# Order of the first loads and first token passes in a SwiGLU feed-forward kernel

## The chip, the core and the metric

The kernel runs on one core of one Trainium2 chip. The core has a matrix engine (TensorE; PE in the profile, with PEld for its weight loads), a vector engine (DVE), a scalar engine (ScalarE, ACT), GpSimd (POOL) and a sync engine (SyncE, SP), each with its own instruction queue. Engines wait for each other by semaphores. SyncE and ScalarE both start DMA transfers here; an issue occupies the queue of the engine that makes it, and the transfer's landing is told by a semaphore of its own. The metric is the device time of one execution in microseconds (us), the median of several.

## The reference

With x of 2048 tokens by D = 512, weights w_gate and w_up of 512 by F = 1376, and w_down of 1376 by 512, all bf16:

```
def reference(x, w_gate, w_up, w_down):
    g = _silu(x @ w_gate)
    u = x @ w_up
    return (g * u) @ w_down
```

## The kernel before

Tokens are worked on in four chunks of 512, F in ten tiles of 128 and a remainder of 96. For each chunk and F tile TensorE makes two groups: G, the tile's columns of w_gate times the tokens, and U, the same of w_up. A group is four accumulating matmuls (D is cut into four parts of 128, index `dk`) into one of eight PSUM banks, used in rotation. ScalarE takes the SiLU of G into a buffer; VectorE multiplies this by U into `hT_sb`, the input of the second product, which follows when all chunks are done. The remainder of F has groups X and Y of its own, and the second product the functions `strips` and what follows it. Neither is touched here.

The weights arrive in slabs of F tiles: (0), (1), (2, 3), (4, 5, 6), (7 to 10). `load_gate` and `load_up` load a slab of w_gate or w_up; in the text wg2 is the gate slab that begins with tile 2, wu2 the up slab. Tokens 0 to 255 are loaded as rows (`load_xn`, two tiles of 128 tokens), transposed by TensorE (`transposes`) and copied from PSUM to `xT_sb` by VectorE and ScalarE in turn, four copies each. All other tokens come by transposing DMAs (`load_x`): x0b brings tokens 256 to 383, x0c 384 to 511, x1 to x3 the other chunks.

SyncE issues nearly all loads, in the written order of `loads_on_sync` (L123): xn0, wu0, wg1, wu1, wg2, wu2, x0b, x0c, wg4, wu4, wg7, wu7, then the rest. ScalarE issues wg0 and xn1 in `loads_on_scalar` (L119), loads its table, and then runs `act_ops` in order (L278); the first four of these are its copies of token tiles 0 and 1, two of each.

TensorE's order is written out by hand, and so is each wait: `gu_needs` (L329) waits for the loads that a pass needs, `gu_step` (L339) issues one matmul over tokens n0 to n1 and, for tokens 0 to 255, waits for the copies. The first eight groups (G0, U0, G1, U1, G2, U2, G3, U3, in the text by kind and F tile; `first` in the code) are cut by tokens, since the tokens of chunk 0 do not come at once:

- warm-up matmuls, transposes of token tile 0, G0 on tokens 0 to 127, transposes of tile 1, U0 on 0 to 127, then G0 and U0 on 128 to 255 (L371 to L378);
- G1, U1, G2, G3, U2, U3 on tokens 0 to 255 (L379);
- G0, U0 on 256 to 383, then on 384 to 511 (L381);
- the other six on 256 to 511 (L384).

From group 8 (G4) on every matmul spans 512 tokens. A G or U group is handed to its reader when its last matmul is done.

Of the kernel before, what the change touches and what calls it, by code (L numbers as in the profile page):

```python
# [14 lines left out]
def bass_standalone__swiglu_ffn__prompt_kernel(nc, x, w_gate, w_up, w_down, out):  # L15
# [3 lines left out]
    KD = D // P  # L19
# [3 lines left out]
    SC = 512  # L23
# [5 lines left out]
    HT = SC // 2  # L29
# [21 lines left out]
    with ExitStack() as es:  # L51
# [32 lines left out]
        def load_sem(name):  # L84
            loads[name] = sem(f"s_{name}")
            return loads[name]
# [6 lines left out]
        def load_x(eng, name, t0, t1):  # L93
            eng.dma_start_transpose(
                xT_sb[:, :, t0:t1], xf[t0:t1, :]
            ).then_inc(load_sem(name), 16)

        def load_w(eng, name, src, base, f0, f1):
            eng.dma_start(
                w_sb[:, :, base + f0:base + f1],  # L100
                src[:, f0:f1].rearrange("(k p) f -> p k f", p=P),
            ).then_inc(load_sem(name), 16)

        slabs = [(0, 1), (1, 2), (2, 4), (4, 7), (7, NFT)]
        slab_of = {ft: a for a, b in slabs for ft in range(a, b)}

        def load_gate(eng, a, b):
            load_w(eng, f"wg{a}", w_gate, 0, a * P, min(b * P, F))

        def load_up(eng, a, b):  # L110
            load_w(eng, f"wu{a}", w_up, UPH, a * P, min(b * P, F - 32))

        def load_xn(eng, i):
            eng.dma_start(xn_sb[:, i, :], xf[i * P:(i + 1) * P, :]).then_inc(load_sem(f"xn{i}"), 16)
# [4 lines left out]
        def loads_on_scalar(act):  # L119
            load_gate(act, *slabs[0])  # L120
            load_xn(act, 1)

        def loads_on_sync(sp):  # L123
            load_xn(sp, 0)
            load_up(sp, *slabs[0])
            for a, b in slabs[1:3]:
                load_gate(sp, a, b)
                load_up(sp, a, b)
            load_x(sp, "x0b", HT, HT + P)
            load_x(sp, "x0c", HT + P, SC)  # L130
            for a, b in slabs[3:]:
                load_gate(sp, a, b)
                load_up(sp, a, b)
            load_w(sp, "wut", w_up, F - (F - 32), F - 32, F)
            for c in range(1, NSC):
                load_x(sp, f"x{c}", c * SC, (c + 1) * SC)
            sp.dma_start(
                wd_sb[:, 0:NFF, :], w_down[0:NFF * P, :].rearrange("(k p) d -> p k d", p=P)
            ).then_inc(load_sem("wd"), 16)
            load_sem("wdt")  # L140
            for y0 in (0, 64):
                sp.dma_start(wd_sb[y0:y0 + 64, T01, :], w_down[NFF * P:F - SR, :]).then_inc(loads["wdt"], 16)
            for x0 in range(0, P, SR):
                sp.dma_start(wd_sb[x0:x0 + SR, T2, :], w_down[F - SR:F, :]).then_inc(loads["wdt"], 16)
            sp.dma_start(wd_sb[0:F_LAST, TAIL, :], w_down[NFF * P:F, :]).then_inc(load_sem("wdl"), 16)
# [7 lines left out]
        def add_group(kind, **what):  # L153
            g = dict(kind=kind, at=len(groups), bank=banks[len(groups) % NB], readers=[], **what)
            groups.append(g)
            return g

        def add_op(eng, g, **what):
            n_read[eng] += 1
            op = dict(g=g, at=n_read[eng], **what)  # L160
            (act_ops if eng == "A" else dve_ops).append(op)
            g["readers"].append((eng, op["at"]))
            return op

        def tview(i, dk):
            return banks[KD * i + dk][:, 0:P // 2].bitcast(BF16)
# [47 lines left out]
        for i in range(NXN):  # L214
            for dk in range(KD):
                eng = "DA"[dk % 2]
                op = add_op(
                    eng, dict(readers=[]), kind="copy", ready=(s_X, KD * i + dk + 1),
                    out=xT_sb[:, dk, i * P:(i + 1) * P], src=tview(i, dk), stored=(None, 0),
                )  # L220
# [12 lines left out]
        for at, t in enumerate(tiles):  # L233
# [3 lines left out]
            for c0, c1 in parts:  # L237
                g = add_group("O", t=t, c0=c0, c1=c1)
                eng = "A" if at % 2 == 1 and c0 == 0 else "D"
                op = add_op(  # L240
                    eng, g, kind="copy", out=o_sb[ob][:, c0:c1], src=g["bank"][:, 0:c1 - c0],
                    stored=(s_out[ob], need),
                )
# [6 lines left out]
        def ready(op):  # L250
            return op["ready"] if "ready" in op else (s_P, op["g"]["at"] + 1)

        def store_tiles(eng, own):
            for o, t, c0, c1, ob, copied, n in stores:
                if o == own:
                    eng.wait_ge(s_A if copied == "A" else s_D, n)
                    eng.dma_start(out_rows(t)[:, c0:c1], o_sb[ob][:, c0:c1]).then_inc(s_out[ob], 16)

        def on_sync(sp):
            loads_on_sync(sp)  # L260
            store_tiles(sp, "S")
            for i in range(NOS):
                sp.wait_ge(s_out[i], 16 * n_store[i])
# [11 lines left out]
        def on_scalar(act):  # L275
            loads_on_scalar(act)
            act.activation(adummy[:, 0:4], zero_c, ACT.Silu)  # L277
            for op in act_ops:  # L278
                act.wait_ge(*ready(op))
                if op["kind"] == "silu":  # L280
                    if op["free"]:
                        act.wait_ge(s_D, op["free"])
                    fn = ACT.Silu
                else:
                    if op["stored"][1]:
                        act.wait_ge(*op["stored"])
                    fn = ACT.Copy
                act.activation(op["out"], op["src"], fn).then_inc(s_A, 1)  # L288
            store_tiles(act, "A")
# [13 lines left out]
        def on_tensor(pe):  # L303
# [25 lines left out]
            def gu_needs(g, n0, n1):  # L329
                c, ft = g["c"], g["ft"]  # L330
                if c > 0:
                    need(f"x{c}")
                if c == 0 and n1 > HT:
                    need("x0b")
                if c == 0 and n1 > HT + P:
                    need("x0c")
                need(("wg" if g["kind"] == "G" else "wu") + str(slab_of[ft]))

            def gu_step(g, dk, n0, n1):  # L339
                c = g["c"]  # L340
                col = (0 if g["kind"] == "G" else UPH) + g["ft"] * P
                if c == 0:
                    for i in range(n0 // P, min(n1 // P, NXN)):
                        after(*xt_ready[i, dk])
                ins = whole(g["bank"], dk, col, c, n0, n1)
                if n1 == SC and dk == KD - 1:
                    ins.then_inc(s_P, 1)

            def gu_matmuls(g, n0, n1):
                gu_needs(g, n0, n1)  # L350
                for dk in range(KD):
                    gu_step(g, dk, n0, n1)
# [17 lines left out]
            first = groups[0:NB]  # L370
# [5 lines left out]
            for dk in range(KD):  # L376
                for g in first[0:2]:
                    gu_step(g, dk, P, HT)  # L378
            for at in (2, 3, 4, 6, 5, 7):  # L379
                gu_matmuls(first[at], 0, HT)  # L380
            for n0, n1 in ((HT, HT + P), (HT + P, SC)):  # L381
                for g in first[0:2]:
                    gu_matmuls(g, n0, n1)
            for g in first[2:]:  # L384
                gu_matmuls(g, HT, SC)

            for g in groups[NB:NO]:
                free(g)
# [98 lines left out]
        on_sync(nc.sync)  # L487
        on_gpsimd(nc.gpsimd)
        on_scalar(nc.scalar)
        on_tensor(nc.tensor)  # L490
        on_vector(nc.vector)

# [27 lines left out]
```

## Time and profile before

| | |
|---|---|
| Median of 3 runs | 120.31 us (120.24 to 120.88) |
| The profiled execution | 119.89 us |
| Its span, first to last instruction | 118.6 us |
| TensorE busy | 115.9 us (98%), 1019 matmuls |
| VectorE busy | 38.0 us (32%) |
| ScalarE busy | 35.1 us (30%) |
| Granted TensorE clock | 1.0 of full |
| DMA moved | 8.83 MB |

The profile is of one execution. A line of a group gives the source line, the engine, the operation and what it writes and reads, then busy time and the idle time before it with what ended it. In the chain of work the path is followed back from the last instruction. In a timeline a row is a start, a duration and what ran, merged where the same instruction repeats; the idle time ahead of it stands in brackets. Matmuls are pipelined: one that follows another starts before the other ends, so that a busy share of 98% does not say that it works at its full rate, and the spacing of the starts says what a matmul costs. The time of a DMA issue (SPq, ACTq) is what it holds its queue, not how long the data take.

### The profile page before, as it was taken

To read this page: it belongs to the slowest core of one execution; us is meant where nothing else is said; L and a number is where in the kernel's file an instruction comes from. 1 tells how busy PE (TensorE), PEld (TensorE's weight loads), DVE (VectorE), ACT (ScalarE), POOL (GpSimd) and SP (SyncE) were. 2 spreads that over 40 slices of the span, in tenths; PEclk is the share of its full clock that TensorE was granted. 3 is DMA by queue.
4 is the path that set the end of the run, shared out by engine and by line. 5 is a ranking of instruction groups with operands and counts; after the bars stand their busy time and mean duration, and the time that the engine had idled before them with its cause. 6 is when DMAs were issued, how large, how long until landed. Compare 5 with 4: busy or idle time off the path is not lost.

```text
span 118.6 us, 2344 instructions
## 1 busy us (share of the span) xinstructions
PE 115.9 (98%) x1019; PEld 59.7 (50%) x1019; DVE 38.0 (32%) x60; ACT 35.1 (30%) x62; POOL 1.1 (1%) x7
## 2 busy tenths in 40 slices
PE   7999999999999999999999999999999999999993
PEld 2788444444444444444444444444444445885442
DVE  0206542444433444324444244360000044003321
ACT  3407334353244272343263432330000033003021
POOL 1000000000000000000000000010000000000000
PEclk9999999999999999999999999999999999999999
DMA  3999999991000000000000000000000017200612
GB/s 87 290 186 336 296 161 221 268 357 25 0 6 0 0 0 0 0 3 3 0 0 6 0 0 0 0 0 6 0 6 0 0 57 237 70 0 6 202 64 88
DMA packets 17642, 8.83 MB, mean 74 GB/s; under 512 B 10624, under 2 KB 17632, under 8 KB 17632
## 3 DMA queue, kind: packets, MB, share of 16 engines
q1 hardware_dynamic: 16816, 8.33, 27.3%
q10 hardware_dynamic: 816, 0.36, 1.1%
q8 instruction: 8, 0.13, 0.5%
q14 instruction: 2, 0.02, 0.0%
HBM read 4.75 MB, written 2.10 MB: 58 GB/s over the span
## 4 chain that ended last, share of the span: by engine, by line
PE 98%; DVE 0%; issue 0%
PE bank L324 62%; PE bank L442 25%; PE bank L481 7%; PE bank L356 2%; PE bank L404 2%; PE bank L365 1%; DVE o_sb L300 0%
## 5 line engine op out<-in xcount | busy, mean ns | idle before, releaser
L324 PE MATMUL bank<-xT_sb,w_sb 128*128 128x512 bf16 (+2 forms) x384 | 73.3, 352 | 0.1
L324 PEld LDWEIGHTS bank<-xT_sb,w_sb 128*128 128x128 bf16 x384 | 36.2, 98 | 36.8 <-DMA w_sb<-in_w_gate_dram 0.3
L296 DVE TENSOR_TENSOR hT_sb<-sg_sb,bank 128x512 bf16<-128x512 f32 x40 | 27.5, 688 | 40.2 <-PE bank L324 39.3
L288 ACT ACTIVATE sg_sb<-bank 128x512 f32<-128x512 f32 x40 | 23.9, 597 | 40.6 <-PE bank L324 40.5
L442 PE MATMUL bank<-wd_sb,hT_sb 32*128 32x512 bf16 x496 | 29.0, 374 | 0.0
L442 PEld LDWEIGHTS bank<-wd_sb,hT_sb 32*128 32x128 bf16 x496 | 15.2, 93 | 11.6 <-issue 0.4
L300 DVE CAST o_sb<-bank 128x512 bf16<-128x512 f32 (+1 forms) x10 | 5.7, 595 | 31.1 <-PE bank L442 25.9
L288 ACT ACTIVATE o_sb<-bank 128x512 bf16<-128x512 f32 (+1 forms) x8 | 4.3, 582 | 33.6 <-PE bank L442 27.9
L481 PE MATMUL bank<-wd_sb,hT_sb 128*128 128x512 bf16 (+2 forms) x56 | 8.1, 304 | 0.0
L481 PEld LDWEIGHTS bank<-wd_sb,hT_sb 128*128 128x128 bf16 x56 | 4.2, 98 | 4.2 <-issue 0.4
L442 PE MATMUL bank<-wd_sb,hy_sb 32*128 32x512 bf16 (+1 forms) x32 | 5.0, 371 | 0.0
L296 DVE TENSOR_TENSOR hx_sb<-sgx_sb,bank 32x512 bf16<-32x512 f32 x4 | 2.8, 692 | 3.5 <-ACT sgx_sb L288 3.5
L288 ACT ACTIVATE sgx_sb<-bank 32x512 f32<-32x512 f32 x4 | 2.4, 588 | 4.5 <-PE bank L324 4.5
L356 PE MATMUL bank<-const-bfloat16-1.0 128*128 128x512 bf16 (+1 forms) x9 | 2.8, 463 | 0.8 <-PEq L505 0.8
L442 PE MATMUL bank<-wd_sb,hx_sb 32*128 32x512 bf16 (+1 forms) x16 | 3.0, 371 | 0.0
L288 ACT ACTIVATE sgy_sb<-bank 64x512 f32<-64x512 f32 x4 | 2.4, 590 | 0.1
L356 PEld LDWEIGHTS bank<-const-bfloat16-1.0 128*128 128x128 bf16 x9 | 1.0, 128 | 2.2 <-issue 2.2
L300 DVE COPY xT_sb<-bank 128x128 bf16<-128x128 bf16 x4 | 0.8, 222 | 4.3 <-PE bank L365 4.3
L404 PE MATMUL bank<-xT_sb,w_sb 128*64 128x512 bf16 x16 | 1.9, 382 | 0.0
L442 PEld LDWEIGHTS bank<-wd_sb,hy_sb 32*128 32x128 bf16 x32 | 1.6, 93 | 0.6
L277 ACT ACT_TABLE_LOAD x1 | 1.3, 1283 | 1.9 <-issue 1.9
L404 PEld LDWEIGHTS bank<-xT_sb,w_sb 128*64 128x64 bf16 x16 | 0.8, 109 | 1.0 <-DVE hT_sb L296 0.4
(15 smaller groups left out, 6.6 us busy)
## 6 DMA issues: line engine op xcount, KB each, us to landing
out_dram<-o_sb SPq DMA_DIRECT2D x15, 128.0 KB, 1.8
wd_sb<-in_w_down_dram SPq DMA_DIRECT2D x1, 1280.0 KB, 7.3
w_sb<-in_w_gate_dram SPq DMA_DIRECT2D x1, 480.0 KB, 5.5
w_sb<-in_w_up_dram SPq DMA_DIRECT2D x1, 448.0 KB, 6.2
w_sb<-in_w_gate_dram SPq DMA_DIRECT2D x1, 384.0 KB, 4.3
w_sb<-in_w_up_dram SPq DMA_DIRECT2D x1, 384.0 KB, 4.7
w_sb<-in_w_up_dram SPq DMA_DIRECT2D x2, 128.0 KB, 3.2
w_sb<-in_w_gate_dram SPq DMA_DIRECT2D x1, 256.0 KB, 3.6
```

The source lines that it names most:

```text
L277: act.activation(adummy[:, 0:4], zero_c, ACT.Silu)
L288: act.activation(op["out"], op["src"], fn).then_inc(s_A, 1)
L296: ins = dve.tensor_tensor(op["out"], op["a"], op["b"], ALU.mult)
L300: ins = dve.tensor_copy(op["out"], op["src"])
L324: return pe.matmul(bank[:, n0:n1], lhsT=w_sb[:, dk, col:col + P], rhs=xT_sb[:, dk, c * SC + n0:c * SC + n1], start=(dk == 0), stop=(dk == ...
L356: pe.matmul(banks[NB - 1][:, 0:width], lhsT=ones_w, rhs=ones_m[:, 0:width], start=True, stop=True)
L365: pe.matmul(tview(i, dk), lhsT=xn_sb[:, i, dk * P:(dk + 1) * P], rhs=ident[:, :], start=True, stop=True, is_transpose=True,).then_inc(s_X, 1)
L404: ins = pe.matmul(g["bank"][y0:y1, :], lhsT=w_sb[:, dk, YC0:YC0 + 64], rhs=xT_sb[:, dk, c * SC:(c + 1) * SC], start=(dk == 0), stop=(dk == ...
L442: ins = pe.matmul(g["bank"][:, 0:c1 - c0], lhsT=h, rhs=wd_sb[r0:r0 + SR, w, c0:c1], start=(start and fk == fks[0]), stop=(stop and fk == f ...
L481: ins = pe.matmul(g["bank"][:, 0:c1 - c0], lhsT=h, rhs=w, start=(last and fk == 0), stop=(fk == (NFF if last else NFF - 1)), skip_group_ch ...
```

## The change

Three parts of one edit. On SyncE, x0b and x0c are issued ahead of wu2, and wg2 is taken off its list. ScalarE issues wg2 between its second and third copy, which are the last of token tile 0 and the first of token tile 1 (its ops are counted from 1, `KD // 2 + 1` is 3). On TensorE, G1 and U1 join G0 and U0 in the passes on tokens 256 to 383 and 384 to 511, and the four groups of tiles 2, 3 run once, on all 512 tokens, in the order G2, U2, G3, U3. The other loads keep their order.

```diff
@@ loads_on_sync
             load_xn(sp, 0)
             load_up(sp, *slabs[0])
-            for a, b in slabs[1:3]:
-                load_gate(sp, a, b)
-                load_up(sp, a, b)
+            load_gate(sp, *slabs[1])
+            load_up(sp, *slabs[1])
             load_x(sp, "x0b", HT, HT + P)
             load_x(sp, "x0c", HT + P, SC)
+            load_up(sp, *slabs[2])
             for a, b in slabs[3:]:
                 load_gate(sp, a, b)
                 load_up(sp, a, b)
@@ on_scalar
             for op in act_ops:
+                if op["at"] == KD // 2 + 1:
+                    load_gate(act, *slabs[2])
                 act.wait_ge(*ready(op))
@@ on_tensor
-            for at in (2, 3, 4, 6, 5, 7):
-                gu_matmuls(first[at], 0, HT)
+            for g in first[2:4]:
+                gu_matmuls(g, 0, HT)
             for n0, n1 in ((HT, HT + P), (HT + P, SC)):
-                for g in first[0:2]:
+                for g in first[0:4]:
                     gu_matmuls(g, n0, n1)
-            for g in first[2:]:
-                gu_matmuls(g, HT, SC)
+            for g in first[4:]:
+                gu_matmuls(g, 0, SC)
```

In the instruction lists TensorE then has 72 G and U matmuls in the first eight groups that are not transposes, where it had 80: 128 tokens wide 48 (before 32), 256 wide 8 (48), 512 wide 16 (0). The other engines' lists differ only by the moved issues.

## Prediction

> **What bounds the kernel now.** I read the chain that ended last first, then the groups, then the timelines of SyncE, ScalarE and the weight loads for the first 12 us, then the table by stage, then the DMA issues. The chain of the profile page:
>
> ```profile
> ## 4 chain that ended last, share of the span: by engine, by line
> PE 98%; DVE 0%; issue 0%
> PE bank L324 62%; PE bank L442 25%; PE bank L481 7%; PE bank L356 2%; PE bank L404 2%; PE bank L365 1%; DVE o_sb L300 0%
> ```
>
> TensorE is the whole path. So the change can pay or cost only through the number of TensorE instructions, their width, and the times at which TensorE stands still for a load. The timeline of the weight loads shows one such stop after the start:
>
> ```profile
> 6.46 6.45 PEld L324 LDWEIGHTS bank<-xT_sb,w_sb 128*128 128x128 bf16 x63 [0.28 <-DMA w_sb<-in_w_gate_dram]
> ```
>
> This is G2, the first work on the gate slab of tiles 2, 3, issued by SyncE at 2.83. The weight load came 0.28 late; since it normally runs beside the matmul before it, the matmuls lose less, which the table by stage gives (window, sum, TensorE busy, clock, DMA share, GB/s; the edges are starts of matmuls, and a count takes in neighbours still in flight):
>
> ```profile
> 5.42:6.30 0.87, 0.87 (x11) 1.00 1.12 331
> 6.46:8.22 1.76, 1.76 (x16) 1.00 1.08 175
> 8.22:9.12 0.89, 0.89 (x18) 1.00 0.66 154
> 9.12:11.73 2.62, 2.62 (x27) 1.00 1.05 339
> ```
>
> The program puts 8, 16, 16 and 24 matmuls in them. A 256-token matmul takes 0.109 us (2.62/24; 0.87/8 agrees), a 128-token one 0.056 (0.89/16). A 512-token one takes 0.216: from 11.73 on, ScalarE's SiLUs follow each other every 1.73 us, 8 matmuls apart. The stop is 6.30 to 6.46, 0.17 us. The clock is full throughout.
>
> The loads' queue, from the SyncE and ScalarE timelines (start, duration of the issue):
>
> ```profile
> 2.83 0.51 SPq L99 DMA_DIRECT2D w_sb<-in_w_gate_dram  x1
> 3.38 0.51 SPq L99 DMA_DIRECT2D w_sb<-in_w_up_dram  x1
> 3.93 2.60 SPq L94 DMA_TRANSPOSE xT_sb<-in_x_dram  x2
> 6.58 0.58 SPq L99 DMA_DIRECT2D w_sb<-in_w_gate_dram  x1
> ...
> 3.68 0.45 ACT L288 ACTIVATE xT_sb<-bank 128x128 bf16<-128x128 bf16 x2 [0.31 <-PE bank L365]
> 4.74 0.45 ACT L288 ACTIVATE xT_sb<-bank 128x128 bf16<-128x128 bf16 x2 [0.61 <-PE bank L365]
> ```
>
> The two transposes hold SyncE 1.3 us each, an ordinary load 0.5. ScalarE is free from 4.13 to 4.74, where the new gate load goes. Last, the DMA issues (KB, us from issue to landing); the two transposes, x0b and x0c, come from windows around their issues:
>
> ```profile
> w_sb<-in_w_gate_dram SPq DMA_DIRECT2D x1, 384.0 KB, 4.3
> w_sb<-in_w_gate_dram SPq DMA_DIRECT2D x1, 256.0 KB, 3.6
> w_sb<-in_w_up_dram SPq DMA_DIRECT2D x1, 256.0 KB, 3.8
> w_sb<-in_w_gate_dram ACTq DMA_DIRECT2D x1, 128.0 KB, 2.8
> ...
> xT_sb<-in_x_dram SPq DMA_TRANSPOSE x1, 4.0
> ...
> xT_sb<-in_x_dram SPq DMA_TRANSPOSE x1, 3.1
> ```
>
> Added to the issue times, wg2 lands at 6.42, wu2 at 7.22, x0b at 7.90, x0c at 8.34, wg4 at 10.92. G2's first matmul starts at 6.46, 0.05 behind its landing.
>
> **The change, part by part.** Up to 6.30 (tiles 0, 1 on tokens 0-255) TensorE runs the same instructions.
>
> Matmuls. Before, from 5.42: 48 of 256 tokens and 16 of 128 tokens, 48 x 0.109 + 16 x 0.056 = 6.14, plus the stop of 0.17, ends at 11.73. After: 8 x 0.109 + 32 x 0.056 + 16 x 0.216 = 0.87 + 1.79 + 3.46 = 6.12, which ends at 11.54 if no load is late. The work itself gains 0.02, the stop 0.17: 0.19 us is all that this change can win. Everything from group 8 on is unchanged.
>
> SyncE's queue. With wg2 gone and wu2 behind the transposes, x0b issues at 2.83 to 4.13, x0c at 4.17 to 5.43, wu2 at 5.47 to 5.98, wg4 at 6.03 instead of 6.58. All later issues come 0.55 us earlier: one load less on this queue.
>
> What is late next, in TensorE's order, with the time by which each load must land to cause no wait (0.05 before its first matmul):
>
> x0b, by 6.25. Before, it landed 0.68 behind the transfer ahead of it (wu2 7.22, x0b 7.90). Now wu1 is ahead, which landed at 5.40, so 6.08: in time. The nearer end is 2.83 + 3.1 = 5.9 (x0c's row), the far end 2.83 + 4.0 = 6.8 (its own row, with wu2 in front), a wait of 0.55.
>
> x0c, by 7.14 (6.30 + 16 x 0.056 - 0.05). From its own row 4.17 + 3.1 = 7.23, a wait of 0.09. The ends: 0.44 behind x0b, as before (6.5), no wait; x0b's row, 8.14, a wait of 1.0.
>
> wg2, by 8.03. ScalarE issues it behind its second copy, 4.03 to 4.13, and 3.6 us (the same load's row) gives 7.7: hidden behind the 128-token passes. With the 384 KB row's 4.3 it would be 8.4, a wait of 0.4. Its issue itself lies in ScalarE's gap: 0.47 to 0.58 us from 4.08 ends by 4.66, before the copy at 4.74. Behind it stand that copy and its neighbour, which feed TensorE's second and fourth step on token tile 1, so without the gap it would cost its length on the path.
>
> wu2, by 8.90 (6.30 + 1.79 + 0.86 - 0.05). This is the load that pays: it leaves SyncE 2.1 us later than before. Its own row, 3.84, gives 9.31. The other near row is wg4's, which was also the first ordinary load behind the transposes: 4.34, less 128 KB at some 330 GB/s (0.39), 3.95, gives 9.42. Rows from the start of the queue (2.8 for 128 KB) give 8.3, no wait; wg4's unscaled gives 9.81. What makes wg4 slow is seen in the table by stage, the last column in GB/s, where the wire is nearly empty around the transposes' landing at 8.34:
>
> ```profile
> 5.90:6.40 0.50, 0.50 (x6) 0.26 (x3) 0.00 (x0) 0.00 (x0) 0.00 (x0) 1.00 1.12 333
> 7.90:8.40 0.50, 0.50 (x9) 0.47 (x7) 0.00 (x0) 0.00 (x0) 0.00 (x0) 1.00 0.86 61
> 8.40:8.90 0.50, 0.50 (x13) 0.50 (x11) 0.00 (x0) 0.00 (x0) 0.00 (x0) 1.00 0.48 120
> ```
>
> That hole moves up with the transposes and then falls on wu2. I take 9.31, wu2's own row, with the scaled wg4 close behind. wg4 and the rest have over 0.5 us: the bytes ahead of them are the same, they issue 0.55 earlier, and wg4 is wanted at 11.5 where it landed at 10.92.
>
> The sum. The last wait sets the end of the first eight groups: x0c would give 7.23 + 0.05 + 0.89 + 3.46 = 11.63; wu2 gives 9.31 + 0.05 + 3 x 0.864 = 11.95, against 11.73: 0.22 us slower. The profiled execution took 119.89 us for a span of 118.6 (1.3 lie around it), so 120.11; it is 0.42 below the median of the runs, and the difference carried to 120.31 gives 120.5.
>
> **A rule weighed.** ScalarE's and SyncE's first issues overlap, 0.81 to 1.28 and 0.81 to 1.21, and took 0.47 and 0.40 us, no longer than SyncE's 0.50 to 0.51 alone, so the rows show no queueing of one behind the other. The Trainium skill, Perfetto Trace Analysis, "DMA Instruction — HWDGE", says that the block that generates descriptors is shared by the two issuing sequencers and locked for exclusive use, and that the issue's recorded time includes the wait for that lock. By it the gate load could stand behind a transpose's issue, and the sum would be rival B's; no row here has an ordinary issue beside a transpose's.
>
> **The rivals.**
>
> A. All loads in time. For it: wg1 landed only 3.1 us after its issue with a full queue, and 256 KB at 333 GB/s need 0.8. Against it: the hole on the wire. End 11.54 to 11.63, 0.1 to 0.2 us faster: 120.1 to 120.2.
>
> B. ScalarE's issue waits for SyncE's transposes. If it is held until x0c's is done (5.43), it ends at 5.93; the copies of token tile 1 start at 5.95 instead of 4.74, and TensorE, which waits for them, is 1.2 us late: 11.54 + 1.21 = 12.75, 1.0 us slower, 121.3. Waits for the loads vanish inside it. It decides (0.6 us) from a hold of 0.8 us on. If the gate load slips in between and x0c is held 0.5 us instead, x0c lands at 7.73 and the end is 12.13: 120.7. Against it: the overlapped first issues.
>
> C. wu2 or x0c at their far ends. wu2 at 9.81 gives 12.45, 0.72 slower; x0c at 8.14 gives 12.54, 0.81 slower: 121.0 to 121.1. It decides from wu2 at 9.70. For it: wg2's bytes now share the engines with the transposes, and wg4's parts landed over 1 us. Against it: wu2 has fewer bytes than wg4.
>
> D. The transposes land no sooner after their issue than before: x0b at 6.8, end 6.8 + 0.05 + 1.79 + 3.46 = 12.10, 120.7. The change would then trade a wait of 0.17 for one of 0.55. Against it: that row had wu2 in front.
>
> **How the numbers follow.** Forecast 0.45, with its own range 120.1 to 120.9 (wu2 between 9.0 and 9.6); A 0.13; D 0.08; B 0.12; C 0.18; something that gains more than 0.5% 0.04, which nothing in the rows offers. Within 0.5% (0.6 us, about what a measurement of this kernel can tell from no change: the three runs lie 0.64 apart) are the forecast, A and D, 0.66; slower are B and C, 0.30; faster 0.04. The range goes from just under A, 120.0, to B, 121.4, and leaves out the unexplained gain and the worst mixtures.
>
> **What would show it.** TensorE's weight loads: no idle at 6.30 if x0b lands by 6.25; 0.1 us near 7.2 for x0c; some 0.4 near 9.0 with the up load named as what ended it; then none. The first 512-token matmul of G2 near 8.2, and group 8 starting near 11.95. ScalarE's DMA issue starting near 4.1 and lasting 0.5, its next copy still at 4.74. I am wrong if that issue lasts 1 us or more, if wu2 lands before 8.9 or after 9.7, or if the transposes' issues lengthen.

## The result, and the profile after

The changed kernel takes 120.85 us in the median of 22 runs (120.47 to 121.34), the kernel before 120.31 (22 runs, 119.84 to 120.88). The ratio is 1.0049, 95% interval 1.0038 to 1.0061: 0.54 us or 0.5% slower, just inside what I had called no change (the interval, 0.38 to 0.61%, reaches to both sides of that line), and 0.35 us above the forecast. The profiled execution took 120.85 us for a span of 119.6, 0.96 more than that of the kernel before, so the two traces differ by more than the medians do. Both numbers need an explanation.

The chain that ended last was all TensorE before. On the page of the changed kernel it reads, by engine and then by line:

```profile
PE 92%; DMA 3%; SPq 3%; issue 0%; DVE 0%
PE bank L326 59%; PE bank L444 25%; PE bank L483 7%; DMA xT_sb<-in_x_dram 3%; PE bank L406 2%; SPq L99 1%; SPq L94 1%; SPq L114 0%; DVE o_sb L302 0%
```

Now a transposing DMA and the SyncE queue up to its issue stand in it. The timeline of the changed kernel gives the place (start, duration, what ran, idle time ahead and what ended it):

```profile
2.83 2.59 SPq L94 DMA_TRANSPOSE xT_sb<-in_x_dram  x2
...
4.06 0.39 ACTq L99 DMA_DIRECT2D w_sb<-in_w_gate_dram  x1
...
5.47 0.58 SPq L99 DMA_DIRECT2D w_sb<-in_w_up_dram  x1
...
8.18 1.44 PEld L326 LDWEIGHTS bank<-xT_sb,w_sb 128*128 128x128 bf16 x20 [0.84 <-DMA xT_sb<-in_x_dram]
...
10.09 2.92 PEld L326 LDWEIGHTS bank<-xT_sb,w_sb 128*128 128x128 bf16 x15 [0.47 <-DMA w_sb<-in_w_up_dram]
```

The stop at 6.30 is gone. In its place TensorE stands before the pass on tokens 384 to 511, until x0c lands at 8.14; by the spacing of its matmuls it loses 0.83 us there. At 10.09 it waits for wu2, and loses 0.14. From then on both kernels run alike: from the end of the first eight groups to the end of the span it is 106.9 us in every trace of this study that is read. So one row tells the whole difference, ScalarE's SiLU of G4 (group 8). In the timeline of the kernel before, and then of the changed one:

```profile
12.80 0.60 ACT L288 ACTIVATE sg_sb<-bank 128x512 f32<-128x512 f32 x1 [0.70 <-PE bank L324]
```

```profile
13.76 0.60 ACT L290 ACTIVATE sg_sb<-bank 128x512 f32<-128x512 f32 x1 [1.13 <-PE bank L326]
```

13.76 - 12.80 = 0.96 us, all of the difference of the two profiled executions. The waits make 0.83 + 0.14 - 0.17 = 0.80 us of it. The other 0.16 us lie ahead of them and are not the change's doing: the changed kernel began G1 at 5.59 us, the kernel before at 5.42, since the token tiles xn0 and xn1, whose loads are issued alike in both, landed at 3.29 and 4.54 instead of 3.13 and 4.37. Another trace of the kernel before (e9, below) has the same lateness and ends its first eight groups no later, as it then has no wait for wg2.

The DMA issues around 4.2 and around 5.6 us of the changed kernel (KB, us from issue to landing) show x0c and wu2:

```profile
w_sb<-in_w_gate_dram ACTq DMA_DIRECT2D x1, 256.0 KB, 3.8
xT_sb<-in_x_dram SPq DMA_TRANSPOSE x1, 4.0
...
w_sb<-in_w_up_dram SPq DMA_DIRECT2D x1, 256.0 KB, 4.6
```

x0c took 4.0 us from its issue, 3.1 before. ScalarE's issue lasted 0.39 us, and x0b landed at 6.05.

One execution now and then is disturbed as a whole and far longer; none of those enters a ratio here, and the profile of one run below (e6) fell on such an execution and is not read.

### The profile page after: what moved, and what is told of

The parts are those of the page before. It is cut to its first block, busy times and chain, and to the rows that moved or that the text cites. A ratio compares the mean times of both kernels' runs of the same rounds, so it can differ in the third digit from the quotient of the medians.

```text
span 119.6 us, 2328 instructions
## 1 busy us (share of the span) xinstructions
PE 116.2 (97%) x1011; PEld 58.3 (49%) x1011; DVE 38.0 (32%) x60; ACT 35.0 (29%) x62; POOL 1.1 (1%) x7
## 4 chain that ended last, share of the span: by engine, by line
PE 92%; DMA 3%; SPq 3%; issue 0%; DVE 0%
PE bank L326 59%; PE bank L444 25%; PE bank L483 7%; DMA xT_sb<-in_x_dram 3%; PE bank L406 2%; SPq L99 1%; SPq L94 1%; SPq L114 0%; DVE o_sb L302 0%
## 5 line engine op out<-in xcount | busy, mean ns | idle before, releaser
L326 PEld LDWEIGHTS bank<-xT_sb,w_sb 128*128 128x128 bf16 x376 | 34.7, 98 | 39.0 <-DMA xT_sb<-in_x_dram 0.8
```

Source lines behind the costliest of these rows:

```text
L326: return pe.matmul(bank[:, n0:n1], lhsT=w_sb[:, dk, col:col + P], rhs=xT_sb[:, dk, c * SC + n0:c * SC + n1], start=(dk == 0), stop=(dk == ...
```

## What the experiments asked

Two theories of x0c's lateness. Theory 1: the gate load on ScalarE's queue, whose data move from 5.1 to 7.3 us, shares the DMA engines with x0c. Theory 2: a transpose issued early behind another is slow by itself. And a question of size: why do the medians differ by 0.54 us and the traces by 0.96?

### e0: the changed kernel once more

No edit.

> The changed kernel once more, for a second trace of it. In its first trace x0c landed at 8.14, 3.98 us after its issue, against 3.06 in the kernel before, and TensorE stood 0.83 us for it. If that is a property of the order of loads (either theory below), x0c lands again 3.7 us or more after its issue, and the wait is 0.5 us or more; if it was the chance of one execution, it lands near 7.2 to 7.5 and the wait is under 0.4. The copy of the gate's issue on ScalarE should again start near 4.05 and last 0.4 to 0.5.

x0c landed at 8.19, 4.0 us after its issue, ScalarE's issue started at 3.99 and lasted 0.39 us. The weight loads waited for the same two loads:

```profile
8.23 1.44 PEld L326 LDWEIGHTS bank<-xT_sb,w_sb 128*128 128x128 bf16 x20 [0.70 <-DMA xT_sb<-in_x_dram]
10.04 2.92 PEld L326 LDWEIGHTS bank<-xT_sb,w_sb 128*128 128x128 bf16 x15 [0.37 <-DMA w_sb<-in_w_up_dram]
```

Both traces show it alike, so it goes with the order of the loads and is not the chance of one execution.

### e1: the gate behind the transposes, on SyncE

```diff
             load_x(sp, "x0c", HT + P, SC)
+            load_gate(sp, *slabs[2])
             load_up(sp, *slabs[2])
@@
-                if op["at"] == KD // 2 + 1:
-                    load_gate(act, *slabs[2])
```

> The gate load wg2 leaves ScalarE and is issued by SyncE behind x0c, ahead of wu2; x0b and x0c keep their places and times of issue. Theory 1 (wg2's 256 KB, on the wire from 5.1 to 7.3 in the changed kernel, share the DMA engines with x0c): x0c has the engines to itself and lands 3.0 to 3.3 us after its issue, 7.2 to 7.5. Theory 2 (a transpose issued early behind another is slow by itself, whatever lies beside it): x0c lands again near 8.1. Either way wg2 now lands late, 9.5 to 10.0 by the row of the load behind the transposes, so TensorE stands 1 to 2 us before G2 and the time is 121 to 122.5 us; the reading is x0c's landing, not the time.

x0c landed at 6.91. The issue, and its landing, in this run's DMA issues:

```profile
xT_sb<-in_x_dram SPq DMA_TRANSPOSE x1, 2.7
```

Theory 2 falls: the same two transposes, issued at the same times, are not slow without the gate beside them. My guess for the time was wrong: 120.55 us in the one execution, not 121 to 122.5. wg2 landed at 8.66, 3.2 us after its issue, not at 9.5 to 10.0, and TensorE waited for no load of weights or tokens after G1 began: in this execution it worked at half pace until about 6.5 us (e8 and e9 below) and came to G2 only at 8.95, after wg2.

### e2: the gate at the start, on ScalarE

```diff
             load_xn(act, 1)
+            load_gate(act, *slabs[2])
@@
-                if op["at"] == KD // 2 + 1:
-                    load_gate(act, *slabs[2])
```

> wg2 is issued by ScalarE at the start, behind xn1, so that it is through before x0c begins. Theory 1: x0c lands by 7.5, the wait before the second pass falls from 0.83 to under 0.4; but 256 KB more now share the wire with wu0, wg1, wu1 (about 0.8 us at 330 GB/s), which come up to 0.8 us later, and x0b stands behind them: a wait of 0.3 to 0.8 moves ahead of G1 or of the first pass on tokens 256 to 383. Time 120.4 to 121.2. Theory 2: x0c still lands 3.9 us or more after its issue, and both waits add up: over 121.

x0c landed at 7.55, 3.4 us after its issue and 0.48 behind x0b; as expected by theory 1, the price moved: wg1 came at 5.82 (5.01 in the changed kernel), wu1 at 6.49 (5.46), x0b at 7.07 (6.05). The ratio to the kernel before is 1.0039 (1.0015 to 1.0063). 256 KB cost the loads beside them 0.8 to 1.0 us here; x0c, 8.14 in the changed kernel and 6.91 in e1, paid 1.2.

### e4: half the gate on ScalarE

```diff
                 if op["at"] == KD // 2 + 1:
-                    load_gate(act, *slabs[2])
+                    load_gate(act, 2, 3)
@@ loads_on_sync, behind x0c
+            load_gate(sp, 3, 4)
             load_up(sp, *slabs[2])
```

(G3 then waits for the half that SyncE issues.)

> The changed kernel with half the gate slab (F tile 2, 128 KB) issued by ScalarE at the same place; the other half (tile 3) goes to SyncE behind x0c. If sharing the engines with the gate load is what holds x0c (8.14 and 8.19 with 256 KB beside it, 6.91 with none), x0c comes in between, 7.3 to 7.8. If it is the mere presence of a second queue beside the transposes, whatever it carries, x0c stays near 8.1; if ScalarE's load does not matter, it comes near 6.9. The time is one look and not the reading.

x0c landed at 7.41, in between as the first theory asks, 3.3 us after its issue:

```profile
xT_sb<-in_x_dram SPq DMA_TRANSPOSE x1, 3.3
```

With 0, 128 and 256 KB beside it on the second queue x0c lands at 6.91, 7.41 and 8.14 or 8.19, at the same time of issue. The lateness goes with the bytes. That shows theory 1 for x0c, as far as the bytes go.

The packets show more. From 5.6 to 6.3 us these are the DMA queues that moved anything (packets, MB, share of the 16 engines), in the changed kernel and then in e1:

```profile
q10 hardware_dynamic: 260, 0.13, 76.6%
```

```profile
q1 hardware_dynamic: 565, 0.14, 109.5%
```

q1 is SyncE's queue, q10 ScalarE's. In the changed kernel SyncE's queue, with x0c on it, stood still from 5.58 to 6.36 us while the gate's data moved (5.65 to 6.32 in e0, and for 0.24 us in e4, with half the gate). The wire was not full in that time: 190 GB/s, against 331 from 5.42 to 6.30 us of the kernel before. So the two loads did not share the engines evenly; x0c's queue paused. Why it pauses, no run here shows.

The Trainium skill, DMA: Bandwidth & Descriptors, "Issuing engines are not separate DMA queues", says that DMAs run on the same 16 engines and interleave whichever engine started them, and that issuing from several saves issue time alone. The three landings agree that a second queue is not a second wire.

### e3: one transpose for tokens 256 to 511

```diff
-            load_x(sp, "x0b", HT, HT + P)
-            load_x(sp, "x0c", HT + P, SC)
+            load_x(sp, "x0b", HT, SC)
@@
-            for n0, n1 in ((HT, HT + P), (HT + P, SC)):
-                for g in first[0:4]:
-                    gu_matmuls(g, n0, n1)
+            for g in first[0:4]:
+                gu_matmuls(g, HT, SC)
```

(The wait for the load x0c, which no longer exists, is taken out too.)

> x0b and x0c become one transposing DMA of 256 tokens, and tiles 0 and 1 take tokens 256 to 511 in one pass. x1 to x3 are 4 times the size of x0b and were issued in 2.4 to 4.6 us, so one issue for 256 tokens should take 1.6 to 2.0 us instead of 2.6 for two. Theory 1: its bytes are on the wire mostly before or beside wg2's; it lands at 6.4 to 7.4, one wait of 0.1 to 1.1 before the pass; wu2 issues 0.6 to 0.9 us earlier and does not make TensorE wait. Time 120.0 to 120.8, faster than the changed kernel. Theory 2 (transposes that follow one another are slow): with only one it lands 3.2 us after its issue plus the longer issue, 6.4 to 6.8, and the time is 120.0 to 120.4.

A miss: 1.0100 (1.0068 to 1.0132), slower than the changed kernel. The issue was shorter as expected (1.85 us instead of 2.6), but the one DMA landed at 7.68, 4.9 us after its issue, again with the gate beside it:

```profile
xT_sb<-in_x_dram SPq DMA_TRANSPOSE x1, 4.9
```

It lands 0.5 us ahead of x0c in the changed kernel, but 1.6 us behind x0b, and the whole pass of 16 x 0.109 = 1.75 us stands behind it, where only 0.89 us stood behind x0c. From its landing the first eight groups take 0.05 + 1.75 + 3.46 us: they end at 12.94, against 12.69 in the changed kernel. I had counted the earlier last byte and not the later first one.

### e5: the gate between the transposes

```diff
             load_x(sp, "x0b", HT, HT + P)
+            load_gate(sp, *slabs[2])
             load_x(sp, "x0c", HT + P, SC)
             load_up(sp, *slabs[2])
@@
-            for n0, n1 in ((HT, HT + P), (HT + P, SC)):
-                for g in first[0:4]:
-                    gu_matmuls(g, n0, n1)
-            for g in first[4:]:
-                gu_matmuls(g, 0, SC)
+            for g in first[0:4]:
+                gu_matmuls(g, HT, HT + P)
+            for at in (4, 6):
+                gu_matmuls(first[at], 0, HT)
+            for g in first[0:4]:
+                gu_matmuls(g, HT + P, SC)
+            for g in first[4:]:
+                gu_matmuls(g, HT if g["kind"] == "G" else 0, SC)
```

(The load on ScalarE is taken out as in e1.)

> All loads on SyncE: wg1, wu1, x0b, wg2, x0c, wu2; TensorE takes tiles 0, 1 on tokens 256 to 383, then G2, G3 on tokens 0 to 255, then tiles 0, 1 on 384 to 511, the rest of G2, G3, and U2, U3 on 512. If a transfer in front of a transpose delays it only by its own bytes, x0b lands by 6.5, wg2 by 7.4, x0c by 8.0 and wu2 by 9.5, each within 0.2 us of its need with a full clock: the first eight groups end at 11.5 to 11.8 against 11.73 before, and the time is the kernel before's within 0.3 us, 120.0 to 120.4. If a transpose is slow whenever an ordinary load is beside it, x0c lands after 8.6 and the time is that of the changed kernel, 120.6 to 121.

x0b landed at 6.05, wg2 at 7.15, x0c at 7.79, wu2 at 9.38, each before its need. TensorE's weight loads run without a stop from 4.6 us on, and the SiLU of G4 comes at 12.66, 0.14 ahead of the first trace of before:

```profile
4.60 8.39 PEld L325 LDWEIGHTS bank<-xT_sb,w_sb 128*128 128x128 bf16 x84
```

```profile
12.66 0.60 ACT L289 ACTIVATE sg_sb<-bank 128x512 f32<-128x512 f32 x1 [1.13 <-PE bank L325]
```

So x0b can go ahead of the gate without harm when the gate waits its turn on the same queue and TensorE's order is fitted to it. The time is that of the kernel before, ratio 1.0011 (0.9984 to 1.0038): what the missing stop can give, at most 0.2 us, is below what these runs tell apart. No version measured over several runs is faster than the kernel before.

### e8 and e9: the kernel before, twice more

No edit.

> The kernel before, for another trace. The part from the first 512-token matmul of group 8 to the end has been 106.9 us in every trace so far, so the median of 120.3 asks for a first part of about 12.1 us where the first trace shows 11.73. Theory: TensorE's pace doubles at a moment that differs between executions, and the kernel before has no wait in which a late moment could hide: with a doubling at 5 us or later its first eight groups end at 12.0 to 12.7, with one before 4 us at 11.6 to 11.8, and the loads are in time for every group but G2. The changed kernel's two traces, with doublings at 3.9 and 5.4, ended them at 12.68 and 12.64. Rival: the kernel before's spread comes from its loads, and a slower execution shows a wait of 0.3 us or more for a load.

> The same kernel and the same expectation as the run ahead of it, since the moment of the doubling is not to be chosen: with two more traces one late doubling is likely.

The SiLU of G4 came at 13.17 in e8 and at 12.80 in e9. Of these 0.37 us 0.25 lie in TensorE's pace at the start: e8 begins G1 at 5.86, e9 at 5.61. The other 0.1 us are a wait for wg2, which landed at 6.79 in e8 and at 6.24 in e9:

```profile
6.83 6.24 PEld L324 LDWEIGHTS bank<-xT_sb,w_sb 128*128 128x128 bf16 x62 [0.22 <-DMA w_sb<-in_w_gate_dram]
```

The rival asked for a wait of 0.3 us or more; it is a third of that. The first eight groups ended at 12.11 in e8, as expected for a doubling at 5 us or later, and at 11.74 in e9, whose doubling at 4.7 lies between the two cases that I had named. The pace itself: in the stretch from 4.6 to 5.4 us the transposes of token tile 1 (groups of instructions by shape: busy us, mean ns of one) read in the first trace of before

```profile
L365 PE MATMUL bank<-ident,xn_sb 128*128 128x128 bf16 x4 | 0.4, 222 | 0.0
```

and in e8

```profile
L365 PE MATMUL bank<-ident,xn_sb 128*128 128x128 bf16 x4 | 0.6, 305 | 0.0
```

The starts of 128-token matmuls stand 0.107 us apart up to some moment and 0.056 after it. That moment is 3.6 us in the first trace of before, 4.0 in the first of the changed kernel, 4.7 in e9, 5.4 in e0 and e8, 6.5 in e1, 6.8 in e2. In e9 it falls among waits for the copies, where the spacing tells little, but the four matmuls of G0 between 4.0 and 4.5 us still took 296 ns each, as in e8, where the first trace of before has 224:

```profile
L324 PE MATMUL bank<-xT_sb,w_sb 128*128 128x128 bf16 x4 | 0.6, 296 | 0.0
```

The clock column of the table by stage does not show the moment. Its rows for the weight loads, first trace of before and then e8, both say 1.00, while twice as many weight loads begin in the one as in the other:

```profile
4.85:5.15 0.30, 0.20 (x6) 1.00 1.21 280
```

```profile
4.85:5.15 0.30, 0.30 (x3) 1.00 1.17 281
```

Four of the traces hold records of the granted clock. The record of the full clock begins at 3.55 us in the first trace of before, at 3.96 in the first of the changed kernel, at 3.77 in e5 and at 8.15 in e7 below, which are the moments that the spacing gives. Ahead of it there is no record, and the column puts 1.00 there; the other traces have none at all. The full clock lasts 116.05 us in the first three and 112.64 in e7, 3.41 us less.

The Trainium skill, TensorE: Matmul & The Clock Gate, "What's actually happening", says that TensorE runs at half its clock until a window of about 3.4 us was busy, that the windows run free of the kernel's start, and that the moment therefore varies by 0.5 us either way. The two paces agree with it (0.107 and 0.056 us for 128 columns), and so does the step of 3.41 us between the recorded lengths; the spread does not, 3.55 to 6.8 us among kernels that start TensorE alike, about one whole window. That a free window causes it was not tried.

### e6, e7 and e10: both kernels without the warm-up matmuls

```diff
-N_WARM = 5
-N_FILL = 2
+N_WARM = 0
+N_FILL = 0
```

The seven matmuls write a bank that no output reads. e6 and e10 are the kernel before with this edit, e7 the changed one.

> The kernel before without its seven warm-up matmuls ahead of the first transposes (work that no output reads). The traces show that TensorE's matmuls double their pace at a moment that differs from run to run (3.6 us in the profile of before, 3.9 in that of the changed kernel, 5.4, 6.4, 6.9 in others). Without warm-up it should come later, at 6.7 to 10. TensorE bounds the kernel before from 3.3 us on, so it should lose about half of the delay: 1.3 to 3 us, 121.6 to 123.3.

> The changed kernel without the same seven warm-up matmuls; the comparison is with e6. Theory: what the change costs is the wait for x0c (landing near 8.15 whatever TensorE does) and a little for wu2; a TensorE that is slow until 7 us or later comes to the pass on x0c after 8.2 and waits for nothing, so the cost vanishes and the two kernels without warm-up agree within 0.2 us, the changed one a shade faster if anything. Rival: the change costs 0.5 us elsewhere (order of banks, ScalarE's issue, later loads), then it stays 0.4 to 0.7 us slower than e6. A second rival, that its loads are late by more than TensorE's delay, would show as a remaining wait for wu2.

> The kernel before without the seven warm-up matmuls, for a trace, since e6 left none that can be read. The changed kernel without them had its doubling at 8.1, no wait for a load, and ended its first eight groups at 13.2. The same doubling here should give 13.0 to 13.4 and no wait for a load, so that the two kernels end level; a doubling 1 us earlier gives some 0.5 us less.

Against the kernel before, e6 stands at 1.0069 (1.0039 to 1.0099), e7 at 1.0086 (1.0057 to 1.0116). Divided by each other the changed kernel is 1.0017 of the other one, 0.2 us where it was 0.54, with an uncertainty of some 0.3 us either way by the spread of the eleven and six runs. So the times alone do not say that nothing is left; that the wait is gone is read from the trace. e6 lost 0.8 us, less than the 1.3 I had named as the least. In e7 x0c landed at 8.40 and wu2 at 10.05, no earlier than in the changed kernel, and TensorE waited for neither:

```profile
4.69 8.40 PEld L326 LDWEIGHTS bank<-xT_sb,w_sb 128*128 128x128 bf16 x69
```

It reached the pass on x0c after the landing, since its pace doubled only at 8.15. e10 doubled at 7.1 and ended its first eight groups at 12.71, below the 13.0 to 13.4 expected for a doubling at 8.1 and within the half us that I had allowed for one a us earlier.

Put together (end of the first eight groups, us, from the spacing of the matmuls):

| Kernel | trace | pace doubles | waits for loads | eight groups end |
|---|---|---|---|---|
| before | first | 3.55 | wg2 0.17 | 11.73 |
| before | e9 | 4.7 | none | 11.74 |
| before | e8 | 5.4 | wg2 0.1 | 12.11 |
| before, no warm-up | e10 | 7.1 | none | 12.71 |
| changed | first | 3.96 | x0c 0.83, wu2 0.14 | 12.69 |
| changed | e0 | 5.4 | x0c 0.69, wu2 0.04 | 12.65 |
| changed, no warm-up | e7 | 8.15 | none | 13.20 |

The kernel before ends when TensorE's pace lets it, but for a small wait for wg2. The changed one cannot end before x0c and wu2 let it, 12.69 and 12.65 in its two traces, whether the pace doubles at 3.96 or 5.4. The cost is 0.95 us for an early doubling (12.69 against 11.73 and 11.74, which the kernel before reaches with a doubling at 3.55 and at 4.7), 0.54 at 5.4 (e0 against e8), and about 0.2, or nothing, without warm-up, at 7 to 8. The measured 0.54 lies between these; how often each start comes up was not measured, so that the medians follow from it is argued and not shown. The runs of the changed kernel still spread over 0.87 us (1.04 before), so its landings, or doublings later than 6 us, must vary the end as well; three traces do not say which.

## Why the prediction was right, and where it was wrong

The forecast of no change beyond 0.5% held by a hair, and 120.85 lies in its own range of 120.1 to 120.9. The way there was in part another one.

- The work of TensorE: 6.12 us without waits, as worked out, and the stop of 0.17 is gone for the reason given. Right. The waits for x0c and wu2 that come on top stand in the places that I had named, but their sizes do not: 0.83 and 0.14, where I had 0.09 and 0.4.
- x0b, said 6.08, landed at 6.05 and made no wait. Right, by the interval to the transfer ahead of it; rival D falls.
- ScalarE's issue, said 4.08 for 0.47 to 0.58 us: 4.06 for 0.39, and 3.99 and 3.90 in e0 and e7, beside SyncE's transposes of 1.28 and 1.26 us, which were no longer than before. Rival B falls. The lock in the Trainium skill (Perfetto Trace Analysis, "DMA Instruction — HWDGE") shows no wait of a size that these rows could tell.
- wg2, said 7.7, landed at 7.84 and was wanted later. Right, but its price was taken in the wrong place: I asked when it would land and not what it would push.
- x0c is the step that failed. I took 3.1 us from its own row before, when no second queue ran beside it, which gave 7.23 and a wait of 0.09; it took 4.0. The far end that I had named, 8.14, is the landing that was measured, and rival C had given the reason in half a sentence, wg2's bytes beside the transposes. e1 and e4 show that reason: by its mechanism rival C came true and not the forecast. It should have been the forecast: as an estimate, 256 KB at the 330 GB/s that the table by stage shows are 0.8 us, and x0c took 0.9 longer than before. The estimate is a price that fits and not the mechanism, since the wire moved 190 GB/s while x0c's queue paused.
- wu2, said 9.31, landed at 10.05 and 10.00. The hole behind the transposes was read rightly, but by these traces the load behind it goes with the transposes' landing, not with its own issue: the next load, where it is 256 KB, landed 1.91, 1.81, 1.75, 1.75, 1.59 and 1.65 us behind x0c (changed, e0, e1, e2, e5, e7), and 1.68 behind the one transpose of e3; issued at 5.46 to 5.48 in the first four and in e7, it landed anywhere from 8.66 to 10.05. With x0c at 8.14 that alone gives 9.9. Since TensorE was already late for x0c, the wait was only 0.14 where I had put 0.4.
- "The clock is full throughout" was wrong. Of the stretch that I had listed, from 5.42 us on, it was true in that one trace. But I read it off a column that says 1.00 also while TensorE runs at half pace, up to 3.55 us in that very trace and beyond 5.42 in others. The first trace of before was one of the fastest executions (119.89, the fastest of 22 is 119.84), doubling at 3.55; I noted that it was 0.42 us below the median and carried a difference between two times over as if they were of one kind. A late doubling makes the kernel before longer (11.74 at 4.7, 12.11 at 5.4), while the changed one hides it in the wait for x0c. The sum was 0.22 us slower, the traces with an early doubling show 0.95, and the median shows 0.54: the forecast came close because the wait was underrated and the cover for it not seen. These two errors work against each other, so that part of the nearness is luck.

## What to carry to other kernels

Here the second issuing engine saved 0.5 us of SyncE's queue and cost the transpose beside it 1.2 us: before a load is moved to it, ask which transfer will be on the engines beside it, and price its bytes on that one. A wait for data costs only what the consumer is early by, so the profile of an execution with a fast start (0.95 us here) overstates it; look at several traces, and compare the spacing of equal instructions at the start before a difference of some tenths of a us is laid on the change. In these traces a load behind a transposing DMA is timed better from the transpose's landing than from its own issue.

## What the runs showed of the hardware

The moment at which TensorE doubles its pace differed by 3.3 us among kernels with the same start (3.55 to 6.8 us); between e9 and e8 of one and the same kernel 0.7 us of it were worth 0.25 us, while the profile's clock column said 1.00 throughout. SyncE's queue, with a transposing DMA on it, paused for 0.7 to 0.8 us beside 256 KB on ScalarE's queue and for 0.24 us beside 128 KB. Behind a transposing DMA the next load of 256 KB landed 1.6 to 1.9 us after the transpose, and an issue of 1.85 us for 256 tokens is shorter than two of 1.3 for 128, but its data came together, and late (7.68).
